# Down-projections in row tiles over four banks, a shorter feature map, and new instruction orders

## The chip, the core and the metric

The kernel runs on one NeuronCore of a Trainium2 chip. Five engines work side by side, each through its own instruction stream in order: TensorE (PE in the profile, its weight loads PEld), VectorE (DVE), ScalarE (ACT), GpSimd (POOL) and SyncE (SP), which issues the DMA transfers. They meet through semaphores. TensorE writes to PSUM, which has eight banks of 128 partitions x 512 fp32 values. The metric is the device time of one execution in microseconds.

## What is computed

One sequence of 2048 tokens of width 512 goes through two branches, which a gate per token mixes. Branch A is attention in four segments of 512 tokens, with 32 heads of width 16 and a memory that is carried from segment to segment; branch B is a gated MLP of width 1792.

```python
g = sigmoid((x * gate_w).sum(-1, keepdims=True))
# branch A, for each of 4 segments, per head (width 16)
p     = softmax(qs @ ks.T * scale + causal mask)
a_dot = p @ vs
phi   = lambda t: where(t > 0, t + 1.0, exp(t))
a_mem = (phi(qs) @ M) / (phi(qs) @ z + 1e-6)
o     = gh * a_mem + (1 - gh) * a_dot          # gh = sigmoid(beta), per head
M, z  = M + phi(ks).T @ vs, z + phi(ks).sum(rows)
a = concat(o) @ wo
# branch B
b = (gelu(x @ w_gate) * (x @ w_up)) @ w_down
out = g * a + (1 - g) * b
```

## The kernel before

**Staging.** All weights are kept in SBUF. Segment s (0 to 3) owns 512 tokens. Its stages are: projections K, Q, V (names `K1_0.2`: segment 1, block 0, piece from contraction block 2 on); gate and up products (`G`, `U`, 14 blocks of 128 features each); scores, exponential and weighted values; the memory; and the down-projection (`D`). A *product* in this document is one matmul of a 128x128 stationary tile with 512 columns. K, Q, V, G, U need four products for a block; a piece is two of them.

**Attention.** Heads lie in four groups of eight; for each tile t of heads (0 to 3), `attention` makes five *fills*: `A0`, `B0`, `A1`, `B1` (two halves of the keys, for the even and the odd head of a pair) and, for even t only, `L` (the low corners). A fill is `qk1_0A0` (segment 1, tile 0, half A, head 0), 8 or 32 matmuls of K=32 in four row groups into the four PSUM banks `X[0..3]` (line 905). One exponential of 128x2048 (`exp…`, ScalarE, line 911) empties the four banks, GpSimd masks the result (`msk…`, line 914), `pv1_0_0` multiplies it with the values in four column tiles, VectorE transposes that (`pvt…`, line 967), and `norm1_0` (lines 979 to 987) divides, transposes and adds it to `oT`. There are 72 fills in all. The memory read of segments 1 to 3, `numx` (line 825), also uses the four X banks in row tiles; `num` adds the last part from `MZbd`; `numd`, `nump`, `numl` (lines 837 to 854) work them up on VectorE, and four transposing DMAs `oTd` bring them into `oT`.

**PSUM.** Four banks are X. The other four (`banks`, names psW) serve everything else: a group of pieces (`Grp`) gets a bank with its first piece and gives it back when its last reader is done.

**Down-projection.** `downs` (line 1056) makes, for each of the four 128-token tiles of a segment, one sum of 18 products: four with `oT` and `wo`, fourteen with `hT` and `wd`. Each sum holds one bank for as long as its pieces `D1_0.0` to `D1_0.16` are spread over the order. `fin` scales by the gate (lines 1098 and 1101) and `out` writes 128 tokens to memory. In the last segment tile 3 uses the X banks instead. `hT` is `gelu(gate) * up`, where `Um` (line 1052) is the multiplication.

**Tile shape.** TensorE runs a product as one 128x128 tile; fills and `numx` as four row tiles of 32x128; `pv` and `mz` as four column tiles. A product that stands between two fills in whose interval a `pv` stands as well is also issued as four column tiles (`column_runs`, line 246, and `mm`, lines 527 to 532: line 530 is the whole product, line 532 the four column tiles).

**Order.** The order on each of the five engines is written out in lists (`ORDER`, line 41). `Sched.schedule` (line 261) walks through these lists, gives out the banks and fixes the order in time; its estimates decide the choice of banks, not the order. `Emitter` turns data dependencies into semaphore waits; a dependency of TensorE on TensorE gets none (lines 390 and 407), because TensorE runs in order.

**Feature map.** `phi_task` (line 722) takes the exponential on ScalarE (line 728, tile `pex`) and then three VectorE steps on 128x1024: `max(t, 0)` (line 731), `min(exp, 1)` (line 733), and their sum (line 735). There are two such tasks for the keys and two for the queries of three segments, twelve in all. **Memory matrix.** `mzbd` masks the accumulated matrix into `MZc` (line 886) and copies its last block in four pieces into the block-diagonal `MZbd` (line 891), whose zeros GpSimd wrote at the start (`consts`, line 653).

Of the kernel before, what the change touches and what calls it, by code (L numbers as in the profile page):

```python
# [26 lines left out]
N_OST = 3  # L27
PSUM_KEYS = ("X", "W")
# [7 lines left out]
DMA_SPARE = 1.6  # L36
LANDING = {
# [67 lines left out]
    ),  # L105
    "dve": (
# [40 lines left out]
class Instr:  # L147
    __slots__ = ("fn", "reads", "writes", "est", "dma_sem", "waits", "deps", "inc", "fence", "wide", "cols")

    def __init__(self, fn, reads=(), writes=(), est=0.1, dma_sem=None):  # L150
# [9 lines left out]
        self.deps = []  # L160
        self.inc = False
        self.fence = False
        self.wide = self.cols = False


class Grp:
# [172 lines left out]
class Emitter:  # L339
# [45 lines left out]
    def finalize(self):  # L385
# [17 lines left out]
        for eng, ins in self.order:  # L403
            req = {}
            for d in ins.deps:
                if d[0] == "c":
                    if d[1] == PE and eng == PE:
                        continue
# [794 lines left out]
```

## Time and profile before

| What | Value |
|---|---|
| Median of 3 runs | 263.48 us (263.07 to 263.88) |
| The profiled execution, its own time | 263.0 us |
| Its span, first to last instruction | 261.8 us |
| TensorE clock granted | 1.00 |
| TensorE busy | 258.5 us, 99% |
| ScalarE busy | 212.2 us, 81% |
| VectorE busy | 195.5 us, 75% |
| GpSimd busy | 105.0 us, 40% |
| The chain that ended last | 97% TensorE |

The busy share of TensorE is not the share in which its array does useful columns: matmuls are pipelined, and their ends in the profile are modelled. In a row of the grouped view, the columns are: line, engine, operation, output<-inputs, shapes, count | busy us, mean ns of one | idle before, and what ended it. In the chain in order of time they are: start, length, piece, all in us. The busy shares in 40 slices show where which engine is loaded; PE stands at 9 nearly throughout:

```profile
PE   8999999999999999999999999999999999999996
PEld 4543445354445434544444444444444434444454
DVE  0789999987988988798896874888874882447543
ACT  3689898999998887988868887688988787768622
```

### The profile page before, as it was taken

Reading aid. Unit: us, or ns where it says so; the run is one execution under the profiler, and the core shown is the slowest. Engines: PE = TensorE matmul, PEld = TensorE weight load, DVE = VectorE, ACT = ScalarE, POOL = GpSimd, SP = SyncE. Lnnn points to the kernel's source line nnn. Section 1 sums busy time; section 2 is a strip of 40 time slices with the busy share of each in tenths; the row PEclk is TensorE's granted clock in tenths of the full one; section 3 lists DMA queues with packets and bytes.
Section 4 is the critical chain, followed back from the end, with each engine's and each line's share of the span. In section 5 each row is a group of like instructions: output and inputs, shape, how many; then the busy total and the mean of one; then the engine's idle time right before and its main releaser. Section 6 shows DMA issues by size and latency. Waiting matters only on the chain.

```text
span 261.8 us, 8784 instructions
## 1 busy us (share of the span) xinstructions
PE 258.5 (99%) x3861; PEld 119.9 (46%) x3861; DVE 195.5 (75%) x371; ACT 212.2 (81%) x185; POOL 105.0 (40%) x256
## 2 busy tenths in 40 slices
PE   8999999999999999999999999999999999999996
PEld 4543445354445434544444444444444434444454
DVE  0789999987988988798896874888874882447543
ACT  3689898999998887988868887688988787768622
POOL 8236760938000183570740171508081045317220
DMA  6992079600009945160000243230001052001002
GB/s 216 325 184 43 4 84 204 222 4 3 0 13 192 263 62 83 27 141 3 0 3 20 48 101 79 24 105 27 18 3 21 3 64 41 3 3 63 23 3 83
DMA packets 32774, 18.33 MB, mean 70 GB/s; under 512 B 20576, under 2 KB 32736, under 8 KB 32736
## 3 DMA queue, kind: packets, MB, share of 16 engines
q1 hardware_dynamic: 31632, 16.73, 30.3%
q10 hardware_dynamic: 1104, 1.05, 1.3%
q8 instruction: 30, 0.49, 0.8%
q14 instruction: 8, 0.07, 0.1%
HBM read 9.84 MB, written 2.10 MB: 46 GB/s over the span
## 4 chain that ended last, share of the span: by engine, by line
PE 97%; DMA 1%; DVE 0%; issue 0%
PE psW L530 59%; PE psW L532 17%; PE psXALL L905 9%; PE psW L953 6%; PE psXALL L532 2%; PE psW L961 1%; DMA hT<-in_A_x_dram 1%; PE psXALL L530 1%; PE psW L872 1%; PE psXALL L825 1%; PE psXALL L632 1%; DVE obf L1084 0%
## 5 line engine op out<-in xcount | busy, mean ns | idle before, releaser
L911 ACT ACTIVATE pt<-psXALL 128x2048 bf16<-128x2048 f32 x64 | 120.1, 1876 | 24.3 <-PE psXALL L905 22.9
L914 POOL TENSOR_SCALAR_AFFINE_SELECT pt<-pt 128x256 bf16<-128x256 bf16 x128 | 57.7, 463 | 91.4 <-ACT pt L911 86.9
L1052 DVE TENSOR_TENSOR hT<-psW,hT 128x512 bf16<-128x512 f32 x56 | 36.7, 681 | 15.7 <-PE psW L530 11.4
L530 PE MATMUL psW<-xT,wg 128*128 128x512 bf16 x192 | 45.7, 379 | 0.0
L530 PE MATMUL psW<-xT,wu 128*128 128x512 bf16 x166 | 41.8, 380 | 0.0
L914 POOL TENSOR_SCALAR_AFFINE_SELECT ptl<-ptl 128x512 bf16<-128x512 bf16 x32 | 23.0, 718 | 44.2 <-ACT ptl L911 42.4
L967 DVE STREAM_TRANSPOSE tb<-psW 128x512 f32<-128x512 f32 x32 | 22.6, 710 | 17.8 <-PE psW L961 17.7
L530 PE MATMUL psW<-wd,hT 128*128 128x512 bf16 x134 | 34.9, 380 | 0.0
L530 PEld LDWEIGHTS psW<-xT,wg 128*128 128x128 bf16 x192 | 18.1, 98 | 21.5 <-issue 0.4
L905 PE MATMUL psXALL<-qT,kpad 32*128 32x320 bf16 (+3 forms) x512 | 25.4, 273 | 0.0
L530 PEld LDWEIGHTS psW<-xT,wu 128*128 128x128 bf16 x166 | 15.1, 98 | 19.1 <-issue 1.9
L532 PE MATMUL psW<-wd,hT 128*32 128x512 bf16 x304 | 20.1, 380 | 0.0
L530 PEld LDWEIGHTS psW<-wd,hT 128*128 128x128 bf16 x134 | 12.5, 98 | 15.6 <-issue 1.7
L953 PE MATMUL psW<-pt,vaug 128*17 128x192 bf16 (+3 forms) x512 | 19.5, 273 | 0.0
L1036 ACT ACTIVATE hT<-psW 128x512 bf16<-128x512 f32 x28 | 15.5, 595 | 4.6 <-PE psW L530 4.6
L905 PEld LDWEIGHTS psXALL<-qT,kpad 32*128 32x128 bf16 x512 | 7.6, 92 | 24.1 <-ACT pt L911 13.6
L812 POOL COPY exsT<-exs 32x4 f32<-32x4 f32 x64 | 14.1, 220 | 8.2 <-ACT exs L803 4.6
L911 ACT ACTIVATE ptl<-psXALL 128x2048 bf16<-128x2048 f32 x8 | 15.0, 1874 | 2.3 <-PE psXALL L905 2.3
L953 PEld LDWEIGHTS psW<-pt,vaug 128*17 128x17 bf16 x512 | 12.2, 91 | 10.0 <-issue 1.2
L530 PE MATMUL psW<-wv,xT 128*128 128x512 bf16 x60 | 16.6, 380 | 0.0
L530 PE MATMUL psW<-xT,wk 128*128 128x512 bf16 (+1 forms) x70 | 15.5, 333 | 0.0
L532 PE MATMUL psW<-xT,wu 128*32 128x512 bf16 x232 | 14.3, 380 | 0.0
(120 smaller groups left out, 358.2 us busy)
## 6 DMA issues: line engine op xcount, KB each, us to landing
out_dram<-ost SPq DMA_DIRECT2D x15, 128.0 KB, 1.9
wg<-in_B_w_gate_dram SPq DMA_DIRECT2D x2, 896.0 KB, 8.1
wu<-in_B_w_up_dram SPq DMA_DIRECT2D x2, 896.0 KB, 6.5
wd<-in_B_w_down_dram SPq DMA_DIRECT2D x2, 896.0 KB, 7.9
phkt<-in_A_x_dram SPq DMA_DIRECT2D x3, 512.0 KB, 5.4
vlow<-vaug SPq DMA_DIRECT2D x8, 136.0 KB, 2.8
hT<-in_A_x_dram SPq DMA_DIRECT2D x2, 256.0 KB, 4.0
wq<-in_A_wq_dram SPq DMA_DIRECT2D x2, 256.0 KB, 5.5
```

Source lines behind the costliest of these rows:

```text
L530: return e.matmul(view(), lhsT, rhs, start=first, stop=last)
L532: r = e.matmul(view()[c:c + 32, :], lhsT[:, c:c + 32], rhs, start=first, stop=last, tile_position=(0, c))
L632: task(f"x0t{nm}_{u}", PE, [Instr(lambda e, k=k, a=a, u=u, k0=k0, src=src: e.transpose(src[:, k, a * 128:(a + 1) * 128], xin[:, 2 * u + a, ...
L812: cross = task(f"exsT{s}", POOL, [Instr(lambda e, g=g, c=c: e.tensor_copy(exsT[sl][32 * g:32 * g + 32, c:16:4], exs[32 * c:32 * c + 32, s4 ...
L825: task(f"numx{s}", PE, [Instr(lambda e, g=g, i=i, qt=qt, t=t: e.matmul(X[g][:, 34 * i:34 * i + 34], phq[32 * g:32 * g + 32, t, qt * 128:(q ...
L905: instrs.append(Instr(lambda e, g=g, lhs=lhs, rhs=rhs, c0=c0, ncol=ncol: e.matmul(X[g][:, c0:c0 + ncol], lhs(32 * g), rhs(32 * g), start=T ...
L911: exp_task(s, f"exp{s}_{t}{name}", [Instr(lambda e: e.activation(dst[:], XALL[:, :].rearrange("p (g c) -> p g c", g=4), ACTF.Exp, scale=AT ...
L914: task(f"msk{s}_{t}{name}", POOL, [Instr(lambda e, view=view, pat=pat, base=base: e.affine_select(out=view, in_=view, compare_op=ALU.is_ge ...
L953: instrs.append(Instr(lambda e, t=t, q=q, kb=kb, slot=slot, c0=c0: e.matmul(gp.f32()[32 * q:32 * q + 17, 128 * kb + 64:512], Vaug[sl][:, k ...
L967: task(f"pvt{s}_{t}_{j}", DVE, [Instr(lambda e: e.transpose(Tb[:, j, :], gp.f32()[:, :]), [gp.key], [("Tb", j)], dve_t(512))], grp=gp)
L1036: lambda e, g=g, ft=ft, s=s: e.activation(hT[s % 2][:, ft, :], g.f32()[:, :], ACTF.Gelu_apprx_tanh),
L1052: task(f"Um{s}_{ft}", DVE, [Instr(lambda e, g=g, ft=ft: e.tensor_tensor(hT[sl][:, ft, :], g.f32()[:, :], hT[sl][:, ft, :], ALU.mult), [g.k ...
```

## The change

1. The down-projections of segments 0 to 2 go through a new function, `row_downs`. For each of the four token tiles the first two products (`D_HEAD`) and the last two (`D_TAIL`) stay whole. Each of the 14 between is cut into four matmuls of K=32, one per row group. Four steps follow each other; in step k row group r works for token tile (r + k) mod 4, so that the four row groups always write four different banks. The first set of steps 1 to 3 waits on TensorE's own semaphore for the previous step's last writes in the same banks (`own`, `hand`), since now two row groups write one bank. All four psW banks are held from the first head to the last `fin`.
2. `phi_task` has two VectorE steps: `max(t, 0) + 1` in one, and the minimum of that and the exponential.
3. `mzbd` makes `MZbd` in one multiplication of the last block with a block mask `blkm`, which GpSimd builds in `consts` (now with five memsets, fenced, and later in GpSimd's order).
4. `ORDER` is new for all engines, and estimates in the schedule are changed. In TensorE's new order the steps `R0.1.2` (segment 0, step 1, from contraction block 2 on; two sets of four) stand in one stretch per segment with fills between them.

The core of the diff:

```diff
+D_HEAD, D_TAIL = 2, 2
...
+    def row_downs(s):
+
+        sl = s % 2
+        gs = tuple(Grp(banks) for _ in range(4))
+
+        def chunk(c, tile):
+            at = slice(tile * 128, (tile + 1) * 128)
+            if c < 4:
+                return oT[sl][:, c, at], wo[:, c, :], [("oT", sl, tile, c), ("w", "wo")]
+            return hT[sl][:, c - 4, at], wd[:, c - 4, :], [("hT", sl, c - 4), ("w", ("wd", (c - 4) // 7))]
+
+        def whole(tile, c0, c1):
+            g = gs[tile]
+            return [mm(g, lambda: g.f32()[:, :], *chunk(c, tile), c == 0, c == 3 + NFT, 512) for c in range(c0, c1)]
+
+        def part(r, tile, c):
+            a, b, rd = chunk(c, tile)
+            return Instr(lambda e: e.matmul(gs[tile].f32()[:, :], a[32 * r:32 * r + 32, :], b[32 * r:32 * r + 32, :],
+                                            start=False, stop=False, tile_position=(32 * r, 0)),
+                         rd, [gs[tile].key], mm_t(512) / 4)
+
+        for tile in range(4):
+            task(f"D{s}_{tile}.0", PE, whole(tile, 0, D_HEAD), grp=gs[tile])
+        c1 = 4 + NFT - D_TAIL
+        for step in range(4):
+            for c in range(D_HEAD, c1, 2):
+                ins = [part(r, (r + step) % 4, cc) for cc in range(c, min(c + 2, c1)) for r in range(4)]
+                t = Task(f"R{s}.{step}.{c}", {PE: ins}, grp=gs)
+                t.tiled, t.row = "qk", True
+                if c == D_HEAD and step > 0:
+                    t.hand = True
+                    for i in ins[:4]:
+                        i.own = True
+                S.add(t)
+        for tile in range(4):
+            task(f"D{s}_{tile}.{c1}", PE, whole(tile, c1, 4 + NFT), grp=gs[tile])
+        for tile in range(4):
+            finish(s, tile, gs[tile])
...
     def downs(s):
+        if not last:
+            return row_downs(s)
...
-                if d[0] == "c" and (d[1] != PE or eng != PE):
+                if d[0] == "c" and (d[1] != PE or eng != PE or ins.own):
...
-                    if d[1] == PE and eng == PE:
+                    if d[1] == PE and eng == PE and not ins.own:
                         continue
...
-            Instr(lambda e: e.tensor_scalar(dst[:, t0:t1, :], src[:, t0:t1, :], 0.0, None, ALU.max), tk, dk,
+            Instr(lambda e: e.tensor_scalar(dst[:, t0:t1, :], src[:, t0:t1, :], 0.0, 1.0, ALU.max, ALU.add), tk, dk,
-            Instr(lambda e: e.tensor_scalar(ex[:], ex[:], 1.0, None, ALU.min), [("pex",)], [("pex",)],
-                  0.5),
-            Instr(lambda e: e.tensor_tensor(dst[:, t0:t1, :], dst[:, t0:t1, :], ex[:], ALU.add),
+            Instr(lambda e: e.tensor_tensor(dst[:, t0:t1, :], dst[:, t0:t1, :], ex[:], ALU.min),
...
-                + [Instr(lambda e, c=c: e.tensor_copy(MZbd[32 * c:32 * c + 32, 34 * c:34 * c + 34],
-                                                      MZc[32 * c:32 * c + 32, 3, :]),
+                + [Instr(lambda e: e.tensor_tensor(
+                    MZbd[:].rearrange("p (c n) -> p c n", c=4), blkm[:],
+                    MZc[:, 3, :].rearrange("p (o n) -> p o n", o=1).to_broadcast([P, 4, 34]), ALU.mult),
```

The new TensorE order around the first row stretch, and its order there before:

```diff
-qk1_0L U1_2.0 V1_2.0 V1_2.2 U1_3.0 U1_2.2 qk1_0A1 U1_3.2 D0_2.0 V2_3.0 V2_3.2 D0_0.0 qk1_0B1 D0_2.2 D0_0.2 U0_10.0 …
+qk1_0L D0_2.0 D0_1.0 D0_3.0 D0_0.0 R0.0.2 qk1_0A1 R0.0.4 R0.0.6 R0.0.8 R0.0.10 R0.0.12 R0.0.14 qk1_0B1 R0.1.2 …
+R0.1.14 qk1_1A0 R0.2.2 … R0.2.14 qk1_1B0 R0.3.2 … R0.3.10 qk1_1A1 R0.3.12 R0.3.14 D0_1.16 D0_2.16 D0_0.16 qk1_1B1
```

More of the change, by code (lines that the diff above doesn't have):

```diff
@@ L36 @@
 DMA_SPARE = 1.6
+OVERLAP = {PE: 0.0, ACT: 0.1, DVE: 0.08, POOL: 0.0, SP: 0.0}
 LANDING = {
@@ L147 @@
 class Instr:
-    __slots__ = ("fn", "reads", "writes", "est", "dma_sem", "waits", "deps", "inc", "fence", "wide", "cols")
+    __slots__ = ("fn", "reads", "writes", "est", "dma_sem", "waits", "deps", "inc", "fence", "wide", "cols", "own")
     def __init__(self, fn, reads=(), writes=(), est=0.1, dma_sem=None):
@@ L162, in __init__ @@
         self.fence = False
-        self.wide = self.cols = False
+        self.wide = self.cols = self.own = False
 class Grp:
@@ L191, in __init__ @@
         self.alts = alts
-        self.grps = () if grp is None else (grp,)
+        self.grps = () if grp is None else grp if isinstance(grp, tuple) else (grp,)
         self.after = tuple(after)
@@ L196, in __init__ @@
         self.tiled = None
+        self.row = self.hand = False
         self.table = None
@@ L259, in column_runs, with change @@
             run = []
+    @staticmethod
+    def change(mode, t):
+        m = "row" if t.row else t.tiled
+        return 0.0 if m == mode else 0.02 if {m, mode} == {"row", "qk"} else SWITCH
     def schedule(self):
@@ L282, in schedule @@
                     continue
-                st = max(cur[e] + (SWITCH if e == PE and t.tiled != mode else 0.0), ready_at[t.id])
+                st = max(cur[e] + (self.change(mode, t) if e == PE else 0.0), ready_at[t.id])
                 if t.grps and t.grps[0].bank is None:
@@ L304, in schedule @@
                     t.finish = st + 2 * t.est[e] if 2 * t.est[e] <= COLD - st else COLD + t.est[e] - (COLD - st) / 2
-                mode = t.tiled
+                mode = "row" if t.row else t.tiled
                 n_ins = sum(8 if i.cols else 2 for i in t.alts[PE])
@@ L313, in schedule @@
                 done += n_ins
-            cur[e] = t.finish
+            cur[e] = t.finish - OVERLAP[e]
             avail = t.finish
@@ L331, in schedule @@
                 npred[s.id] -= 1
-                hop = 0.0 if (e == PE and s.alts.keys() == {PE}) else HOP[e]
+                hop = 0.0 if e == PE and s.alts.keys() == {PE} and not (t.row and s.hand) else HOP[e]
+                if e in (ACT, DVE) and s.alts.keys() == {e}:
+                    hop = 0.02
                 ready_at[s.id] = max(ready_at[s.id], avail + hop)
@@ L477, in _build @@
     MZbd = sb("mzbd", [P, 136])
+    blkm = sb("blkm", [P, 4, 34])
     ident = sb("ident", [P, 128])
@@ L652, in _build @@
          bias=3000.0)
-    task("consts", POOL, [
-        Instr(lambda e: e.memset(MZbd[:], 0.0), writes=[("MZbd",)], est=0.2)]
+    cons = task("consts", POOL, [
+        Instr(lambda e: e.memset(blkm[:], 0.0), writes=[("c", "blk")], est=0.2)]
+        + [Instr(lambda e, c=c: e.memset(blkm[32 * c:32 * c + 32, c, :], 1.0), [("c", "blk")], [("c", "blk")], 0.1)
+           for c in range(4)]
         + [Instr(lambda e, j=j: e.tensor_copy(bdmask[:, j, :], maskc[j][:, 0:1].to_broadcast([P, 17])),
                  [("c", "mask", j)], [("c", "bd", j)], 0.2) for j in range(2)], bias=100.0)
+    for ins in cons.alts[POOL]:
+        ins.fence = True
     exp_tasks = [[] for _ in range(NSEG)]
@@ L730, in phi_task @@
         task(f"{nm}c{s}_{i}", DVE, [
-            Instr(lambda e: e.tensor_scalar(dst[:, t0:t1, :], src[:, t0:t1, :], 0.0, None, ALU.max), tk, dk,
+            Instr(lambda e: e.tensor_scalar(dst[:, t0:t1, :], src[:, t0:t1, :], 0.0, 1.0, ALU.max, ALU.add), tk, dk,
                   0.5),
-            Instr(lambda e: e.tensor_scalar(ex[:], ex[:], 1.0, None, ALU.min), [("pex",)], [("pex",)],
-                  0.5),
-            Instr(lambda e: e.tensor_tensor(dst[:, t0:t1, :], dst[:, t0:t1, :], ex[:], ALU.add),
-                  dk + [("pex",)], dk, 0.79)])
+            Instr(lambda e: e.tensor_tensor(dst[:, t0:t1, :], dst[:, t0:t1, :], ex[:], ALU.min),
+                  dk + [("pex",)], dk, 0.76)])
     def klow_tasks(s, tiles):
@@ L748, in klow_tasks @@
                 ACT: [Instr(lambda e, dst=dst, src=src, j=j: e.activation(dst, src, ACTF.Copy, scale=maskc[j][:, 0:1]),
[L749 removed]
+                            rd, wr, 0.29 + n / 880.0)],
                 DVE: [Instr(lambda e, dst=dst, src=src, j=j: e.tensor_scalar(dst, src, maskc[j][:, 0:1], None, ALU.mult),
@@ L763, in prep @@
                                                               None, ALU.mult),
-                          [("kT", t), ("c", "mask", j)], [("kpad", j, t)], dve_t(512, 4, ap=True))
+                          [("kT", t), ("c", "mask", j)], [("kpad", j, t)], 0.53)
                     for j in ((1,) if first else (0, 1))])
@@ L793, in prep @@
             xt[:, 0:4, :], xt[:, 0:4, :], gwb[:].rearrange("p (o d) -> p o d", o=1).to_broadcast([P, 4, D]),
-            ALU.mult), xkeys + [("w", "gwb")], xkeys, 1.22)])
+            ALU.mult), xkeys + [("w", "gwb")], xkeys, 1.32)])
         for a in range(4):
@@ L819, in prep @@
             exsT[sl][:].rearrange("p (o b) -> p o b", o=1).to_broadcast([P, 8, 16]), ALU.mult),
-            [ek] + [("c", "omgT", g) for g in range(4)], [("GdT", sl)], 0.3)])
+            [ek] + [("c", "omgT", g) for g in range(4)], [("GdT", sl)], 0.38)])
         if s > 0:
@@ L827, in prep @@
                 MZc[32 * g:32 * g + 32, t, :], start=True, stop=True, tile_position=(32 * g, 0)),
-                [("phq", t), ("MZc",)], [("X", g)], 0.0086)
+                [("phq", t), ("MZc",)], [("X", g)], 0.0076)
                 for i, (qt, t) in enumerate(parts[:15]) for g in range(4)]).tiled = "qk"
@@ L843, in prep @@
                          [gn.key, ("exr", s)], [("nd",)], 0.24),
-                   Instr(lambda e: e.reciprocal(ndsc[:], ndsc[:]), [("nd",)], [("nd",)], 0.4)], grp=gn)
+                   Instr(lambda e: e.reciprocal(ndsc[:], ndsc[:]), [("nd",)], [("nd",)], 0.93)], grp=gn)
             ok = phkt[:].rearrange("p a (t h e) -> p (a t) h e", t=4, e=16)
@@ L875, in memory @@
                     start=(kt == 0), stop=(kt == 3), tile_position=(0, 32 * c)),
-                    [("phkt", t), ("Vaug", sl, kt)], [gm.key], 0.0115)
+                    [("phkt", t), ("Vaug", sl, kt)], [gm.key], 0.0079)
                 for t in range(4) for kt in range(4) for c in range(4)], grp=gm)
@@ L890, in memory @@
                 [("MZc",)], 0.33)]
-                + [Instr(lambda e, c=c: e.tensor_copy(MZbd[32 * c:32 * c + 32, 34 * c:34 * c + 34],
-                                                      MZc[32 * c:32 * c + 32, 3, :]),
-                         [("MZc",)], [("MZbd",)], 0.2) for c in range(4)])
+                + [Instr(lambda e: e.tensor_tensor(
+                    MZbd[:].rearrange("p (c n) -> p c n", c=4), blkm[:],
+                    MZc[:, 3, :].rearrange("p (o n) -> p o n", o=1).to_broadcast([P, 4, 34]), ALU.mult),
+                    [("MZc",), ("c", "blk")], [("MZbd",)], 0.28)])
     pt_next = [0]
@@ L907, in fill @@
                             tile_position=(32 * g, 0)), rd, [("X", g)],
-                            (0.018 / len(steps) + ncol / 2370.0 + (0.01 if ncol < 128 else 0.0)) / 4))
+                            (0.006 / len(steps) + ncol / 2370.0 + (0.006 if ncol < 128 else 0.0)) / 4))
                 last_qk[s] = task(f"qk{s}_{t}{name}", PE, instrs)
@@ L967, in pv @@
                 task(f"pvt{s}_{t}_{j}", DVE, [Instr(lambda e: e.transpose(Tb[:, j, :], gp.f32()[:, :]),
-                                                    [gp.key], [("Tb", j)], dve_t(512))], grp=gp)
+                                                    [gp.key], [("Tb", j)], 0.71)], grp=gp)
             def norm():
@@ new lines, in finish @@
+    def finish(s, tile, g):
+        gt = 4 * s + tile
+        ost = ostage[gt % N_OST]
+        rd, wr = [g.key, ("omgt", s)], [("ost", gt % N_OST)]
+        f = S.add(Task(f"fin{s}_{tile}", {
+            ACT: [Instr(lambda e: e.activation(ost[:], g.f32()[:, :], ACTF.Copy, scale=omgt[:, gt:gt + 1]), rd, wr,
+                        act_t(512, ap=True))],
+            DVE: [Instr(lambda e: e.tensor_scalar(ost[:], g.f32()[:, :], omgt[:, gt:gt + 1], None, ALU.mult), rd, wr,
+                        dve_t(512, ap=True))]}, grp=g))
+        if s == NSEG - 2:
+            fins.append(f)
+        dma(f"out{gt}", SP, lambda: out[0, gt * 128:(gt + 1) * 128, :], lambda: ost[:], wr, [("hbm", gt)], 131072,
+            issue=0.47, sm=sem_out[gt])
@@ L1095, in downs @@
             pieces(f"D{s}_{tile}", g, ins, 2, after=dep)
-            rd = [key, ("omgt", s)]
-            f = S.add(Task(f"fin{s}_{tile}", {
-                ACT: [Instr(lambda e, view=view, gt=gt, tile=tile: e.activation(
-                    ostage[(4 * s + tile) % N_OST][:], view(), ACTF.Copy, scale=omgt[:, gt:gt + 1]), rd,
-                    [("ost", (4 * s + tile) % N_OST)], act_t(512, ap=True))],
-                DVE: [Instr(lambda e, view=view, gt=gt, tile=tile: e.tensor_scalar(
-                    ostage[(4 * s + tile) % N_OST][:], view(), omgt[:, gt:gt + 1], None, ALU.mult), rd,
-                    [("ost", (4 * s + tile) % N_OST)], dve_t(512, ap=True))]}, grp=g))
-            if s == NSEG - 2:
-                fins.append(f)
-            dma(f"out{gt}", SP, lambda gt=gt: out[0, gt * 128:(gt + 1) * 128, :],
-                lambda tile=tile: ostage[(4 * s + tile) % N_OST][:], [("ost", (4 * s + tile) % N_OST)], [("hbm", gt)], 131072, issue=0.47, sm=sem_out[gt])
+            finish(s, tile, g)
     fins = []
```

1 line of the change is left out of this document (removed), and 164 rows, old and new, of the table ORDER.

## The prediction

> **What bounds the kernel now.** I read the busy shares and the chain of waits first, then TensorE's waits, then the chain in order of time, which gives the prices of TensorE's work.
>
> ```profile
> PE 258.5 (99%) x3861; PEld 119.9 (46%) x3861; DVE 195.5 (75%) x371; ACT 212.2 (81%) x185; POOL 105.0 (40%) x256
> PE 97%; DMA 1%; DVE 0%; issue 0%
> engine line waited for: us in total, times, longest us
> PE psW L623 <- PEq L1188: 0.8, 1, 0.8
> PE psXALL L632 <- DMA hT<-in_A_x_dram: 0.3, 1, 0.3
> ```
>
> TensorE is busy for 258.5 of 261.8 us and carries 97% of the chain. Its own waits add up to 1.1 us, all in the head. So work taken from VectorE, ScalarE or GpSimd buys nothing by itself; only TensorE's own time counts, and any new wait of TensorE is paid in full. A busy TensorE need not be computing, so I look at the chain in order of time (start, length, piece), where score fills alternate with projections:
>
> ```profile
> 88.28 2.27 PE psW L530 x10
> 90.55 0.33 PE psXALL L905 x8
> 90.88 2.70 PE psW L530 x12
> ...
> 205.45 0.33 PE psXALL L905 x8
> 205.78 2.27 PE psW L530 x10
> 208.05 0.34 PE psXALL L905 x32
> 208.39 2.26 PE psW L530 x10
> 210.65 0.33 PE psXALL L905 x8
> ```
>
> Twelve products take 2.70 us and ten 2.27, so one 512-column product costs 0.215. From 205.45 to 208.05 is one period of 2.60 us: ten products (2.15) and a fill. A fill is 512 columns in four row tiles at once. Were it as fast as a product's 512 columns it would cost 0.215. That leaves 2.60 - 2.15 - 0.215 = 0.235 us, in which no column flows. The tile shape changes twice per period (128x128 to four row tiles of 32x128, and back), so **one change of shape costs about 0.117 us**. That the row tiles do flow at the product's rate is borne out by the fill of 32 small matmuls: eight sets of 64 columns, with four times the weight loads, take 0.34 against 0.33.
>
> Counting shape changes in TensorE's order of instructions before, I get 150: 72 fills and 3 memory reads (line 825) are 75 stretches of row tiles, each entered and left. 150 x 0.117 is 17.6 us, the only sizeable part of TensorE's time that is not columns.
>
> **The change part by part.**
>
> Row tiles for the down-projections. Per segment 0 to 2, 16 full products stay (the first two and last two of each tile's 18) and 56 become 56 sets of four K=32 matmuls: same columns, 168 sets in all. I count the same 1530 column groups (single products or concurrent sets) before and after. What goes is shape changes. In the new order 5, 5 and 6 fills stand inside the three row stretches, so 16 row stretches become 3: 75 become 62, and the changes 150 become 124. 26 x 0.117 = **-3.0 us**.
>
> A row set that *adds* into four banks at once is not in the trace: fills start fresh sums. Its cost is bounded by rows: zero extra from the fills above; the other end is an adding set in another tiling, here 72 column tiles, 18 sets:
>
> ```profile
> 78.07 4.00 PE psW L532 x72
> ```
>
> 4.00/18 is 0.222, so at most 0.007 more per set, 1.2 us for 168. I take zero, because the fills share tiling, banks and weight loads. The Trainium skill ("TensorE: Matmul & The Clock Gate", "Part 3: Packing small matmuls — row/col tiling") speaks against this: it gives a measured speedup of 3.07 for four row tiles at N=512, not 4. By that each set would cost 0.215 x 4/3.07 = 0.28, an estimate from that page, and 168 sets 11 us more; the fills here do not show it.
>
> Hand-overs. In each of the three later steps the first set waits for TensorE's own last write of those banks (nine times). TensorE runs in order, so everything behind waits too, the next fill and thus ScalarE's exponentials included. No row has such a self-wait; the nearest is how soon ScalarE sees a fill finish:
>
> ```profile
> 23.75 0.40 PE L905 MATMUL psXALL<-qT,kpad 32*128 32x320 bf16 x8
> 24.20 1.88 ACT L911 ACTIVATE pt<-psXALL 128x2048 bf16<-128x2048 f32 x1 [0.23 <-PE psXALL L905]
> ```
>
> 0.45 after the fill's start, thus 0.45 - 0.215 = 0.235 after its last column. In eight of nine places a fill (0.215) stands between the last set and the waiting one, so 0.02 to 0.04 stays: **+0.25 us**. Ends: 0 and 9 x 0.235 = 2.1. The cover is the fill; in the ninth place (segment 2, second to third step) there is none, but there the exponential is waited for anyway.
>
> The exponential loop. All scores share one set of four banks, so the next fill waits for the exponential of the last. Its floor:
>
> ```profile
> 44.10 1.87 ACT L911 ACTIVATE ptl<-psXALL 128x2048 bf16<-128x2048 f32 x1
> 46.02 0.40 PE L905 MATMUL psXALL<-qT,kpad 32*128 32x448 bf16 x8
> ```
>
> The exponential ended at 45.97 and the fill began 0.05 later, so the loop is at least 0.45 + 1.88 + 0.05 = 2.38 us. Before, the usual period of 2.60 hid it. A row period with ten sets is 2.15 + 0.215 = 2.37, level with the floor (seven of them: +0.1). Shorter ones stall: the one after the fill 3_0A1 (tile 0, half A, second head of the pair) has eight sets, 1.94, +0.44; the one after 3_2L has eight products, 1.72 + 0.215 + 0.235 = 2.17, +0.21. Other ScalarE work between exponentials overlaps its neighbours by 0.1 and fits into the 12- and 14-set periods. Together **+0.75**; ends 0.55 (a floor 0.05 lower at the last two, nothing at the seven) and 1.45 (0.07 more at ten places where two copies stand between exponentials).
>
> Entry to the row stretches. Four open sums hold all four working banks for 16 products and 56 sets, so nothing can interleave except fills, and the stretch needs the last norm and the last gated product of its segment, both VectorE's:
>
> ```profile
> L1052 DVE TENSOR_TENSOR hT<-psW,hT 128x512 bf16<-128x512 f32 x56 | 36.7, 681 | 15.7 <-PE psW L530 11.4 <-PE psW L532 3.8 <-ACT hT L1025 0.3
> L967 DVE STREAM_TRANSPOSE tb<-psW 128x512 f32<-128x512 f32 x32 | 22.6, 710 | 17.8 <-PE psW L961 17.7
> L983 DVE TENSOR_TENSOR obf<-tb,sc 128x512 bf16<-128x512 f32 x16 | 12.4, 775 | 0.5
> L985 DVE STREAM_TRANSPOSE ott<-obf 128x512 bf16<-128x512 bf16 x12 | 8.5, 711 | 0.4
> L987 DVE TENSOR_TENSOR oT<-oT,ott 128x512 bf16<-128x512 bf16 x12 | 6.1, 506 | 0.7
> L979 DVE RECIPROCAL recip<-tb 128x32 f32<-128x32 f32 x16 | 5.5, 343 | 0.1
> L981 DVE TENSOR_TENSOR sc<-recip,gdT 128x32 f32<-128x32 f32 x16 | 3.5, 221 | 0.6
> L771 DVE TENSOR_SCALAR kpad<-kT,maskc 128x1024 bf16<-128x1024 bf16 x12 | 5.8, 494 | 0.0
> L750 DVE TENSOR_SCALAR klow<-kT,maskc 128x1024 bf16<-128x1024 bf16 x4 | 3.1, 799 | 0.0
> ```
>
> A norm is 0.34 + 0.22 + 0.78 + 0.71 + 0.51 = 2.56 us, in segment 0 without the last. I add up both sides for each entry. Segment 0, from fill 1_0A0: the product pv0_3_0 and its way to VectorE 0.9; a transpose 0.71, seven gated products 4.8, a pad 0.5, two low keys 1.6 and the norm 2.05, together 10.5. TensorE has 24.7 products' worth, ten more, two fills and the four head pairs before its first row set: 42.7 x 0.215 + 3 x 0.215 + 5 x 0.117 = 10.4, so it is level; back-to-back steps overlap a little in the trace, so I charge nothing. Segment 1, from the end of pv1_3_0: VectorE needs 0.24 + 0.71 + 2.56 + 2 x 0.68 = 4.9 until the last bank is free, TensorE gets there after 24 products and a fill, 5.6: in hand. Segment 2, from the end of pv2_3_0: 0.24 + 0.71 + 0.49 + 0.65 + 2.56 + 2 x 0.68 = 6.0 against 26 products and a fill, 5.9: **+0.1**. Ends: 0, and one 0.68 step late at each entry, 2.0.
>
> The queues. SP now issues the first half of wd behind two transposing transfers, which wait for the last step of line 849 on VectorE:
>
> ```profile
> 60.18 0.33 PE psXALL L905 x8
> ...
> 66.18 11.66 ACT L1025 ACTIVATE hT<-hT 128x2048 bf16<-128x2048 bf16 x5
> ...
> 191.10 0.56 PE psXALL L825 x60
> ...
> L849 DVE TENSOR_TENSOR phkt<-psXALL,ndsc 128x480 bf16<-128x480 f32 x12 | 7.6, 650 | 0.1
> ...
> 76.90 2.53 SPq L563 DMA_TRANSPOSE oT<-phkt  x2
> ...
> wd<-in_B_w_down_dram SPq DMA_DIRECT2D x2, 896.0 KB, 7.9
> q8 instruction: 30, 0.49, 0.8%
> ```
>
> Counted from fill 0_3B1 (60.2 before): the large GELU pieces began 6.0 after it, and one copy fewer (0.5) now stands ahead, so two pieces of 1.8 end at 9.1. VectorE then has four gated products, three steps of line 849 and two pads, 5.7, to 14.8. SP's two transfers take 2.5 and wd 7.9: 25.2. TensorE reaches fill 1_0A0 after 64.5 products, a fill and a memory read, 15.0, the row stretch 10.4 later and the first set that reads wd two sets and a fill on, 26.0: nil, with 0.8 in hand. TensorE's matmuls grow from 3861 to 4674, 21%; the instruction queue held 0.8% of 16 engines' span for 30 blocks, 37 would be 1%, and TensorE's waits show none for code: nil.
>
> VectorE's steps. The feature map loses one of three steps (0.525 x 12), the memory matrix four copies for one multiply (12 x 0.173 against 3 x about 0.28):
>
> ```profile
> L733 DVE TENSOR_SCALAR pex<-pex 128x1024 bf16<-128x1024 bf16 x12 | 6.3, 525 | 0.0
> L891 DVE COPY mzbd<-mzc 32x34 bf16<-32x34 bf16 x12 | 2.1, 173 | 0.4
> L886 DVE TENSOR_TENSOR mzc<-mzacc,gbd 128x136 bf16<-128x136 f32 x3 | 0.9, 284 | 0.0
> ```
>
> 6.3 + 2.1 - 0.85 = 7.5 us off VectorE, hidden behind TensorE: nil on the path. GpSimd's constants, four memsets more and moved behind the masks of tile 2, are wanted only before the first memory read, a tile later: nil.
>
> Sum: -3.0 + 0.25 + 0.75 + 0.1 = **-1.9 us**, 261.8 to 259.9 in span. The profiled run took 263.0 with 1.2 us around the span, 0.48 below the median of 263.48, so I take it off the median: 263.48 - 1.9 = **261.6**.
>
> **The rivals.**
>
> *Each row set pays the 0.007 and the hand-overs are dear (no change).* For: neither is in a row. Against: the fills' rate. With hand-overs at half their upper end (+0.8): 261.6 + 1.2 + 0.8 = 263.6: fewer changes of shape, but no gain.
>
> *The entries cost more than the shapes save (slower).* Place: the start of each row stretch, where TensorE has no other work because every bank is held. A norm late by its 2.56 us at all three: +7.7, 269.2; late by 1.6 each: 266.3. It decides from (1.9 + 0.8)/3 = 0.9 us each. For: segments 0 and 2 have nothing in hand by my count, and wd 0.8. Against: VectorE is rid of 7.5 us, and before, all of VectorE's order left TensorE without a wait.
>
> *Adding in four banks runs at a lower rate (slower).* The dearest that a row shows for 512 columns in row tiles is the fill's whole piece of 0.33, with its two changes in it; at that price per set, 168 x 0.115 = +19: 280.9. It decides from 2.7/168 = 0.016 per set. For: no row shows it. Against: fills, and column tiles that do add. The Trainium skill's 3.07 (page and section above) would put it at 272.6, as an estimate.
>
> **How the numbers follow.** Forecast 0.69 (own range 260.4 to 262.7), no change 0.13, late entries 0.12, lower rate 0.06. 0.3% of 263.5 is 0.8 us, about what can be told from no change. Faster 0.69, same 0.13, slower 0.18. The range: low end all stalls nil, 263.48 - 3.0 = 260.4; high end the hand-overs at their upper end (2.1 in place of 0.25) and one late entry (0.7), 261.6 + 1.9 + 0.7 = 264.2.
>
> **What would show it.** Inside a row stretch the fill and sets follow without the 0.117 gap, periods of 2.38 to 2.40 with ten sets; 124 changes; TensorE's waits stay near 1 us plus 0.6 at fills 3_0B1 and 3_2A1; first sets of a step no more than 0.05 late. Sets above 0.23, or gaps of a microsecond before a row stretch, would prove me wrong.

## The result, and the profile after

The changed kernel takes 262.06 us (median of 22 runs) against 263.44 us for the kernel before on the same chip (22 runs): a ratio of 0.9952, interval 0.9937 to 0.9966, so 0.9 to 1.7 us faster. The profiled executions span 260.8 us after and 261.8 us before.

The head of the profile of the changed kernel, and its chain of waits by engine:

```profile
span 260.8 us, 10397 instructions
PE 254.2 (97%) x4653; PEld 127.0 (49%) x4674; DVE 184.2 (71%) x348; ACT 212.2 (81%) x190; POOL 104.6 (40%) x260
...
PE 90%; ACT 3%; DVE 2%; issue 2%; DMA 1%; POOL 1%; ACTq 0%; POOLq 0%
```

TensorE's share of the chain has gone from 97% to 90%; ScalarE and VectorE now stand in it. VectorE is busy 184.2 us in place of 195.5: its two shorter parts alone make that 187.8 (e3_dve_alone below), and the rest comes from the new lists, which also move 44 small tasks (copies, sums, scalings) between ScalarE and VectorE, 21 of them to VectorE and 23 to ScalarE. Of 4674 matmuls 4653 have a record; the missing ones are mostly first products after a stretch of another shape, and the chain shows each as "0.16 issue", which is no idle time.

The chain in order of time (start, length, piece) through the first row stretch of the changed kernel. Line 917 is a fill, line 1085 the row sets, four matmuls each:

```profile
84.85 0.22 PE psXALL L917 x8
85.06 2.59 PE psW L1085 x48
87.65 0.22 PE psXALL L917 x8
87.87 3.13 PE psW L1085 x56
...
94.29 0.22 PE psXALL L917 x8
94.51 2.20 PE psW L1085 x40
```

Twelve sets take 2.59, so a set that adds into four banks costs 0.216, no more than a whole product, and a fill among them costs 0.22 where it cost 0.33 between products. Fourteen sets after a hand-over (87.87) take 3.13 in place of 3.02. So the row tiles do in the trace what they were to do. The other end of the matter is segment 2:

```profile
206.30 0.22 PE psXALL L917 x8
206.51 2.16 PE psW L1085 x40
208.67 0.33 PE psXALL L917 x32
209.00 2.18 PE psW L1085 x40
211.18 0.24 PE psXALL L917 x8
211.43 0.94 PE psW L1085 x16
212.36 0.01 issue
212.38 1.10 PE psW L1085 x16
213.48 0.39 PE psXALL L917 x8
```

At 212.38 stands the hand-over that no fill covers, at 213.48 fill 3_0B1. Two times four sets are 1.73 by the price above; they take 0.94 and 1.10, and the fill 0.39: 0.26 of that is the hand-over, 0.23 the wait for the exponential. The dearest wait in segment 3, at fill 3_2A1, has ScalarE itself in the chain:

```profile
232.31 0.40 PE psXALL L917 x32
...
232.80 1.89 ACT ptl L923
234.69 0.05 issue
234.73 0.40 PE psXALL L917 x8
```

**One number for each run.** The traces differ in their heads: the first fill starts between 13.29 and 13.82 us in the changed kernel and its variants, through the first loads. So I add up, for each trace and from the first fill on, the time from the start of each of TensorE's column groups to the start of the next, less 0.2133 us per 512 columns (columns without a record are counted too). All kernels here have the same columns, so differences of this sum are differences of time. How far two traces agree shows e5_whole_seg2, which has the changed kernel's code up to the row stretch of segment 2: each fill up to there starts within 0.01 us of its twin. Where the expectations below quote such sums, they count from the end of the head and come out up to 0.23 higher (3.55 for 3.32, 0.69 for 0.62, 0.82 for 0.75).

Before, the sum is 21.52 us, after 20.61: **0.91 less**. 26 changes of shape fewer at 0.103 (the median gap at a change in the trace of before; row tiles to products 0.103, products to row tiles 0.099, column tiles to row tiles 0.108) make 2.7, so 1.8 us went elsewhere. Each trace is one execution: those of the kernel before and of e3_dve_alone lie 0.5 and 0.6 us below the medians of their runs, that of the changed kernel 0.1. What the old orders usually lose beyond that stands in no trace here, so comparisons with these two are given by the ratios as well (the medians differ by 1.4 us, the traces by 0.9).

### The profile page after: what moved, and what is told of

The parts are those of the page before. It is cut to its first block, busy times and chain, and to the rows that moved or that the text cites. A ratio compares the mean times of both kernels' runs of the same rounds, so it can differ in the third digit from the quotient of the medians.

```text
span 260.8 us, 10397 instructions
## 1 busy us (share of the span) xinstructions
PE 254.2 (97%) x4653; PEld 127.0 (49%) x4674; DVE 184.2 (71%) x348; ACT 212.2 (81%) x190; POOL 104.6 (40%) x260
## 4 chain that ended last, share of the span: by engine, by line
PE 90%; ACT 3%; DVE 2%; issue 2%; DMA 1%; POOL 1%; ACTq 0%; POOLq 0%
PE psW L539 34%; PE psW L541 24%; PE psW L1085 14%; PE psXALL L917 8%; PE psW L965 5%; ACT pt L923 2%; PE psXALL L541 2%; DMA hT<-in_A_x_dram 1%; PE psXALL L539 1%; PE psW L973 1%; DVE tb L979 1%; ACT ptl L923 1%; PE psXALL L836 1%; DVE hT L1064 0%; PE psXALL L641 0%
## 5 line engine op out<-in xcount | busy, mean ns | idle before, releaser
L1085 PE MATMUL psW<-wd,hT 32*128 32x512 bf16 x576 | 34.8, 374 | 0.0
L539 PE MATMUL psW<-xT,wu 128*128 128x512 bf16 x111 | 28.1, 380 | 1.2 <-issue 0.8
L1114 DVE TENSOR_SCALAR ost<-psW,omgt 128x512 bf16<-128x512 f32 x8 | 5.8, 747 | 32.7 <-PE psW L539 31.1
L539 PE MATMUL psW<-xT,wg 128*128 128x512 bf16 x112 | 28.0, 380 | 0.6 <-issue 0.3
L541 PE MATMUL psW<-xT,wu 128*32 128x512 bf16 x424 | 25.9, 379 | 0.0
L541 PE MATMUL psW<-xT,wg 128*32 128x512 bf16 x432 | 25.4, 379 | 0.0
L1085 PEld LDWEIGHTS psW<-wd,hT 32*128 32x128 bf16 x576 | 18.9, 93 | 10.5
L539 PEld LDWEIGHTS psW<-xT,wg 128*128 128x128 bf16 x116 | 10.5, 98 | 13.0 <-issue 2.1
L541 PEld LDWEIGHTS psW<-xT,wu 128*32 128x32 bf16 x424 | 10.8, 97 | 10.4 <-issue 0.4
L541 PEld LDWEIGHTS psW<-xT,wg 128*32 128x32 bf16 x432 | 10.6, 97 | 10.0 <-issue 0.4
```

Of the source, the lines that this page charges most:

```text
L539: return e.matmul(view(), lhsT, rhs, start=first, stop=last)
L541: r = e.matmul(view()[c:c + 32, :], lhsT[:, c:c + 32], rhs, start=first, stop=last, tile_position=(0, c))
L1085: return Instr(lambda e: e.matmul(gs[tile].f32()[:, :], a[32 * r:32 * r + 32, :], b[32 * r:32 * r + 32, :], start=False, stop=False, tile_ ...
L1114: DVE: [Instr(lambda e: e.tensor_scalar(ost[:], g.f32()[:, :], omgt[:, gt:gt + 1], None, ALU.mult), rd, wr, dve_t(512, ap=True))]}, grp=g))
```

## The experiments

All ratios are against the kernel before, run on the same chip; "beyond columns" is the sum just described. A ratio difference of 0.001 is 0.26 us.

| Run | Ratio (interval) | Beyond columns, us |
|---|---|---|
| before | | 21.52 |
| changed | 0.9952 (0.9937 to 0.9966) | 20.61 |
| e1_whole | 1.0066 (1.0054 to 1.0078) | 23.93 |
| e2_dve_undone | 0.9985 (0.9974 to 0.9997) | 21.63 |
| e3_dve_alone | 1.0008 (0.9989 to 1.0027) | 21.47 |
| e4_more_waits | 1.0057 (1.004 to 1.0074) | 23.23 |
| e5_whole_seg2 | 0.9972 (0.9955 to 0.9989) | 21.23 |
| e6_whole_seg0 | 0.9981 (0.9963 to 0.9999) | 21.36 |
| e9_whole_seg1 | 0.9971 (0.9949 to 0.9992) | 21.21 |
| e7_moved | 0.998 (0.9963 to 0.9997) | 21.61 |
| e8_whole_mz | 1.0056 (1.0034 to 1.0078) | 23.75 |
| e11_norm_late | 1.0032 (1.0014 to 1.005) | 22.94 |

**Row sets as whole products (e1_whole).**

```diff
-                ins = [part(r, (r + step) % 4, cc) for cc in range(c, min(c + 2, c1)) for r in range(4)]
-                t = Task(f"R{s}.{step}.{c}", {PE: ins}, grp=gs)
...
+                S.add(Task(f"R{s}.{step}.{c}", {PE: whole(step, c, c + 2)}, grp=gs))
```

> The changed kernel with its own orders, in which every piece of two row sets is issued as two whole products (128x128 tile) in the same place, so that each step does one tile; no self-wait. 150 changes of tile shape in place of 124, same columns. Theory (the gain is the changes of shape, part of it lost again to waits): 26 changes x 0.103 us (the median gap at a change in the trace of before) = +2.7, less the hand-overs (0.6) and the stalls of the ten-set and eight-set periods (0.4) that go with the row tiles: +1.7, so 263.8 us. That is above the kernel before, because the new orders have waits of their own (about 0.5). Rival (the gain comes from VectorE's shorter steps or from the new orders, row tiles are neutral): 262.1 us, as the changed kernel.

Measured: 265.24 us against 263.6 for the kernel before, 3.32 us more beyond columns than the changed kernel. Both theories missed it, the first by 1.4 us. The chain of this run at the third memory matrix (line 883, 64 small matmuls):

```profile
171.97 0.34 PE psXALL L917 x32
172.31 0.59 PE psW L883 x57
172.91 1.29 issue
174.20 0.22 PE psW L883 x6
```

In the midst of these matmuls, with no semaphore to wait for, TensorE stands still; 1.46 us more than in the changed kernel lie there. Without that piece the sum is 22.47, 1.86 above the changed kernel, and the forecast of +1.7 is near. The runs by segment and e8_whole_mz test that reading.

**Segment by segment (e5_whole_seg2, e6_whole_seg0, e9_whole_seg1).** The same edit under `if s == 2:`, `s == 0` and `s == 1`.

> The changed kernel with whole products in place of the row sets in segment 2 alone (six fills stand inside that stretch: 10 changes of shape come back, 134 in all). Theory: 10 x 0.103 = +1.03 us, less what the row tiles lose there (the uncovered hand-over 0.25, two covered ones 0.07, stalls of the exponential loop 0.09 + 0.03 + 0.23): +0.35 in the profiled span, 262.4 us; so segment 2 gains little. Rival (row tiles are worth a third of what the first run showed in every segment, 3.2 / 3): +1.1, 263.1 us.

> The same in segment 0 alone (five fills inside: 8 changes come back, 132 in all). Theory: 8 x 0.103 = +0.82, less three covered hand-overs (0.11) and 0.06 of the exponential loop: +0.65, 262.7 us. Rival as for segment 2: +1.1, 263.1 us. TensorE's instructions after this stretch stand 168 earlier in its code, so a stop for code like the 1.3 us one of the first run may appear at another place; then it is read off the trace and taken out.

> Whole products in place of the row sets in segment 1 alone (five fills inside the stretch: 8 changes of shape come back, 132 in all). Theory: 8 x 0.103 = +0.82, less two covered hand-overs seen late there (0.07) and the stall of 0.17 at fill 2_0L: +0.6 in the span from the end of the head on, 262.7 us; with the runs of segments 2 and 0 (+0.69 and +0.82 from the head on) the row tiles are then worth 2.1 us, and 3.55 - 2.1 = 1.45 of the first run is the stop without a releaser. Rival (the first run's 3.2 is all the row tiles'): the three segments have to add up to 3.5, so +2.0 here, 264.1 us.

Measured: +0.62, +0.75 and +0.61 beyond columns, together 1.98 (1.8 by the ratios), with no such stop in any of them (0.09 and 0.03 of the last two lie at the third memory matrix, behind the stretch). The first run's 3.32 less its stop is 1.86, and its fills come 0.66, 0.57 and 0.62 later in the three stretches. So **the row tiles are worth 1.9 us**, not 3.2, and the rival that all of the first run's difference is theirs falls. Segment 2 comes back with 0.27 more than I expected; the chain of e5_whole_seg2 shows where:

```profile
211.78 0.36 PE psXALL L917 x8
...
212.22 1.89 ACT pt L923
214.11 0.05 issue
214.16 0.40 PE psXALL L917 x8
```

The period of eight products in that place waits for the exponential as well, 0.28 beyond a plain change of shape; I had counted that wait as one that goes with the row tiles.

**The stop (e8_whole_mz).**

```diff
-qk2_2L mz2 U2_11.0 U2_9.0 U2_11.2 U2_3.0 qk2_2A1 Q3_2.0
+qk2_2L U2_11.0 U2_9.0 U2_11.2 U2_3.0 qk2_2A1 mz2 Q3_2.0
```

(and VectorE's `mzacc2` three tasks later.)

> The first run of this study (all row sets as whole products) with the third memory matrix's 64 small matmuls one fill later, so that TensorE has 1.7 us more work in the stretch of code before the place where it stood still for 1.3 us without a releaser. Theory (TensorE waited for its code there, which belongs to the place of those matmuls in the code, not to the row tiles): the gap is gone, 265.2 - 1.4 = 263.8 us, so that row tiles are worth 1.7. Rival (the 3.2 us belong to the row tiles): 265.2 us.

Measured: 264.92 us. The stop at the third memory matrix is gone, but the time isn't: the moved matmuls brought waits for ScalarE. Its waits and its chain:

```profile
PE psW L541 <- ACT qT L559: 0.6, 1, 0.6
PE psXALL L917 <- ACT ptl L923: 0.2, 1, 0.2
```

```profile
176.95 0.50 ACT qT L559
177.45 0.04 issue
177.50 1.05 PE psW L541 x16
```

So the stop went when the small matmuls were moved, as expected, and the price of the row tiles rests on the three runs by segment, not on this one. That TensorE waited for its own code there is argued only: an instruction transfer ran between 171.4 and 171.6 in the trace of e1_whole, but none while TensorE stood still (172.9 to 174.2), and no row says that TensorE waited for it. The trace of e8_whole_mz also has a shorter stop, 0.4 us at 109.74, ahead of the second memory matrix, where the same code in e1_whole runs through. So the place in the code is not the whole story, and the cause of these stops stays open.

**VectorE's two parts (e3_dve_alone, e2_dve_undone).** The first puts the two-step feature map and the one-step memory matrix into the kernel before; the second takes them out of the changed kernel.

```diff
-            Instr(lambda e: e.tensor_scalar(dst[:, t0:t1, :], src[:, t0:t1, :], 0.0, 1.0, ALU.max, ALU.add), tk, dk,
+            Instr(lambda e: e.tensor_scalar(dst[:, t0:t1, :], src[:, t0:t1, :], 0.0, None, ALU.max), tk, dk,
...
+            Instr(lambda e: e.tensor_scalar(ex[:], ex[:], 1.0, None, ALU.min), [("pex",)], [("pex",)],
...
-            Instr(lambda e: e.tensor_tensor(dst[:, t0:t1, :], dst[:, t0:t1, :], ex[:], ALU.min),
+            Instr(lambda e: e.tensor_tensor(dst[:, t0:t1, :], dst[:, t0:t1, :], ex[:], ALU.add),
```

> The kernel before with VectorE's two parts alone (feature map in two steps, memory matrix in one, GpSimd's constants for it), orders as before. Theory: no change, 263.4 us, within 0.3. Rival (VectorE's steps give the gain): 262.1 us.

> The changed kernel with the feature map in three VectorE steps and the memory matrix in four copies again: 7.5 us more on VectorE, the rest and all orders unchanged. Theory (VectorE's steps are hidden behind TensorE): no change, 262.1 us, within 0.3. Rival (the shorter steps are what lets the row stretches start without a wait): waits of TensorE of 0.5 to 2 us ahead of the row stretches, 262.6 to 264 us.

Measured: in the old orders the parts are worth nothing (ratio 1.0008, 0.05 less beyond columns). In the new orders they are worth 1.02 (0.9 by the ratios). TensorE's program is the same in e2_dve_undone and in the changed kernel, so the start of each matmul can be set against its twin; the lag (behind the head, where it is 0.03) grows in these places:

```
matmul                                    changed   e2     lag
value product of segment 1, after 0_3B1    58.85   59.03   0.18
up product of segment 0                    65.19   65.67   0.48
fill 1_1A0                                 90.77   91.48   0.71
up product of segment 1, after 1_3A0      115.76  116.60   0.84
gate product of segment 2                 124.67  125.65   0.99
```

No single wait is large, and none stands where I had looked for it, at the entry of a row stretch. At fill 1_1A0, inside the first row stretch, ScalarE's rows show the way, first in e2_dve_undone, then in the changed kernel:

```profile
88.60 1.06 ACT L742 ACTIVATE pex<-kT 128x1024 bf16<-128x1024 bf16 x1 [0.89 <-DVE kT L749]
89.56 1.86 ACT L925 ACTIVATE pt<-psXALL 128x2048 bf16<-128x2048 f32 x1
...
87.41 1.06 ACT L741 ACTIVATE pex<-kT 128x1024 bf16<-128x1024 bf16 x1
88.37 1.86 ACT L923 ACTIVATE pt<-psXALL 128x2048 bf16<-128x2048 f32 x1
```

The feature map's exponential writes the tile `pex`, which VectorE's last step of the task before (line 749) still reads. With three steps in place of two that step ends later, ScalarE waits 0.89 us for it, the score exponential behind starts 1.19 us later, and fill 1_1A0 has to wait for that one. The theory is right for the orders before and wrong for the new ones, which spend what VectorE was relieved of.

**The price of a hand-over (e4_more_waits).**

```diff
-                if c == D_HEAD and step > 0:
+                if c == D_HEAD + 2 or c == D_HEAD and step > 0:
                     t.hand = True
```

> The changed kernel with a wait for TensorE's own last write at the second piece of each of the 12 steps as well, 12 waits more, with nothing between the write and the wait. It prices an uncovered hand-over. By the one uncovered hand-over of the changed kernel (0.25 us late): 12 x 0.25 = +3.0, less the exponential's stalls that these waits now cover (0.4): 264.7 us. By the upper end of the prediction (0.235): 264.5. Rival (a hand-over costs 0.04 with or without cover, and the late set there was the exponential loop's): 262.1 + 0.5 = 262.6 us.

Measured: 265.06 us, +2.63 beyond columns. The fills behind a self-wait with nothing between come 0.23 later each (1_1A0, 1_1B0, 2_0B0, 3_0B0), so **0.23 for each uncovered self-wait**. Not all twelve are uncovered: `R0.0.4` stands behind fill 1_0A1 and costs 0.08, and the one ahead of fill 3_0B1 falls into the wait for the exponential and adds 0.07. The chain of this run at the first of them in segment 1:

```profile
143.52 0.58 PE psW L1085 x8
144.10 0.01 issue
144.11 0.70 PE psW L1085 x8
```

Two pieces of two sets, 0.43 each without a wait, take 0.59 and 0.71 here. The rival (0.04 with or without cover) falls. In the changed kernel the eight covered hand-overs are late by 0.00 to 0.04 and 0.23 together.

**The entries (e11_norm_late).**

```diff
+                if t == 3 and s < 3:
+                    ins[2:2] = [Instr(lambda e: e.tensor_tensor(ov, tv[:, :, :, 0:16], rb, ALU.mult),
+                                      [("Tb", 0), ("Tb", 1), ("sc1", i2)], [("obf",)], 0.79) for _ in range(2)]
```

> The changed kernel with the large multiplication of the norm of the last tile done three times in segments 0 to 2, so that VectorE comes 2 x 0.73 = 1.46 us later to what each row stretch waits for; the result is the same. In the changed kernel's trace VectorE is done 0.7, 0.5 and 0.3 us before TensorE needs it at the three entries (segments 0, 1, 2). Theory (a late VectorE is paid in full there, since every bank is held and nothing else can run): 0.75 + 0.95 + 1.15 = +2.85, 264.9 us, with the waits ahead of or in the whole products that open the stretch. Rival (the margins are larger than they look, since VectorE has idle time ahead): +0.3 or less, 262.4 us.

Measured: +2.33 beyond columns. TensorE's waits of this run:

```profile
PE psW L539 <- DVE hT L1067: 0.6, 1, 0.6
PE psW L539 <- DVE qT L562: 0.4, 1, 0.4
PE psW L1088 <- DVE oT L997: 0.4, 1, 0.4
```

All three lie at the entries: the norm itself in segment 0 (line 997 into 1088), the banks behind it in segments 1 and 2. The lag against the changed kernel grows by 0.58, 0.79 and 0.96 there. Of 1.46 us each, 0.9, 0.7 and 0.5 were therefore in hand; past that, a late VectorE is paid in full.

**Two waits taken out by order (e7_moved).**

```diff
-exp2_0A0 pke2_0 exp2_0B0 pke2_1 exp2_0L exp2_0A1
+exp2_0A0 exp2_0B0 pke2_0 exp2_0L pke2_1 exp2_0A1
...
-qk3_2A0 U3_5.0 U3_0.0 U3_0.2 U3_6.0 U3_5.2 U3_6.2 pv3_0_0 qk3_2B0 pv3_0_1 D2_3.16 pv3_1_1 pv3_1_0 qk3_2L U3_4.0
+qk3_2A0 D2_3.16 U3_5.0 U3_0.0 U3_0.2 U3_6.0 U3_5.2 qk3_2B0 U3_6.2 pv3_0_0 pv3_0_1 pv3_1_1 qk3_2L pv3_1_0 U3_4.0
```

(`fin2_3` goes ahead of `exp3_2B0`, and `Um3_4` behind `pvt3_1_0`.)

> The changed kernel with two waits of TensorE for ScalarE taken out by order alone: in segment 2 the two exponentials of the feature map go behind one score exponential more (fill 2_0L was 0.17 late), and in segment 3 the last output copy of segment 2 and its products go ahead of the second tile's exponential, with the product of pt and V one fill later (fill 3_2A1 was 0.31 late). Theory (each wait is on the path): -0.45, 261.6 us, and both fills start without a wait. Rival (the time is lost again at the next wait, since ScalarE's work is what limits there): 262.1 us.

Measured: 1.00 us more beyond columns than the changed kernel, nearly all of it between fills 3_2A0 and 3_2A1. ScalarE's and TensorE's rows of this run, in the view in order of time:

```profile
230.64 1.88 ACT L921 ACTIVATE pt<-psXALL 128x2048 bf16<-128x2048 f32 x1 [1.55 <-PE psW L963]
233.78 1.88 ACT L921 ACTIVATE ptl<-psXALL 128x2048 bf16<-128x2048 f32 x1 [1.26 <-PE psW L971]
...
232.57 0.41 PE L915 MATMUL psXALL<-qT,klow 32*128 32x64 bf16 x32 [0.83 <-ACT pt L921]
```

The exponentials now wait for `pv` (lines 963 and 971), which has to read the old contents of `pt` and `ptl` before they can be written anew: I had moved `pv` later without counting whose buffer it frees. The other half changed nothing: fill 2_0L is still 0.17 late, because exponential 2_0B0 had waited for its fill, not for the feature map's exponential ahead of it. No version tried here beats the changed kernel.

## Why the prediction was right, and where its size was off

- **Changes of shape, -3.0: right, a little too large.** 124 changes and no gap inside a stretch, as forecast. A change costs 0.103, not 0.117, so -2.7: I had divided all 0.235 us of a period that were not columns by its two changes, though some 0.04 of them belong to the fill's second set (0.013) and to the 0.003 that every product takes beyond its columns. The Trainium skill ("TensorEngine Tiling (Array Packing)", "Key Properties") says that a change of tiling mode drains TensorE. The trace has a gap of 0.10 us at each change, which fits it.
- **Adding sets at no extra: right.** 0.216 each. The rival of a lower rate and the Trainium skill's 3.07 ("TensorE: Matmul & The Clock Gate", "Part 3: Packing small matmuls — row/col tiling"), by which a set would take 0.28 (an estimate), are not borne out here. The upper end of 0.222 was read a little too high: the 4.00 us of the 72 column tiles hold a change of shape, and without its 0.10 a set there takes 0.217.
- **Hand-overs, +0.25: right.** 0.23 for the eight covered ones; an uncovered one costs 0.23, the upper end of 0.235 that I had taken from ScalarE's row. The ninth was to cost nothing of its own, since the exponential is waited for anyway: at fill 3_0B1 hand-over and wait make 0.26 + 0.23 = 0.49, where the prediction had 0.44 for the exponential loop.
- **The exponential loop, +0.75: right in place, too small.** 0.49 there, 0.31 at fill 3_2A1 (0.21 forecast), and 0.36 in the ten-set periods (0.1 forecast): 1.16 in all, inside the ends of 0.55 to 1.45. The floor of 2.38 is what one gets when ScalarE starts 0.45 after the fill; where the fill has itself waited, and after an `L` fill of 32 matmuls, the starts of the fills in segment 2's stretch (206.13, 208.56, 211.03, 213.48) are 2.43 to 2.47 apart. That is the term that was mis-sized most among those I priced.
- **Entries, +0.1: nil**, with 0.9, 0.7 and 0.5 us in hand. The mechanism of the rival "late entries" is real (paid in full past the margin) but does not set in; the count had put the margins at 0, 0.7 and -0.1.
- **The queues, nil: right.** The trace of the changed kernel has no wait of TensorE for `wd` or for code.
- **VectorE's steps, nil: right as an addition to the old orders, wrong in the new.** The forecast of 7.5 us off VectorE holds (7.7 in e3_dve_alone), but in the new orders these steps cover 1.0 us of waits. The prediction's reason, that TensorE's waits of before show none for VectorE, holds only for the orders of before.
- **What the sum left out: the new orders away from the row stretches.** By the traces, e3_dve_alone to e1_whole without its stop is 21.47 to 22.47, +1.0 for the orders alone. By the ratios it is +0.1 (-0.5 to +0.7), since the traced execution of e3_dve_alone lies below its median; so their cost is known only to lie between these bounds. The prediction charged them only fill 3_2A1. In the changed kernel I find, beyond the terms above, fills 0_3A1 (+0.16) and 1_0B0 (+0.10) and three smaller ones (0.04 to 0.05) late behind ScalarE, and a product late behind VectorE by 0.11: 0.5 in all. Ahead of 0_3A1 ScalarE started an exponential 0.82 after its fill in place of 0.45; the profile names GpSimd's line 693, which now runs there. In e2_dve_undone, where GpSimd runs the same work 0.3 us later, that exponential is on time and the next one starts 0.81 after its fill. So the delay goes with GpSimd's work, but what it waits for stays open.

Added up: -2.7 + 0.2 + 1.2 + 0.5 = -0.8, against -0.91 in the trace (waits of before that are gone make up part of the rest), where the prediction had -1.9. By undoing, the row tiles with their waits are worth 1.9; the prediction's own terms for them (-3.0, 0.25, 0.54 of the loop, 0.1) give 2.1. So the forecast of the main edit held.

The whole came out at -1.4 us by the medians, near the forecast of -1.9, and that is in part luck. Without VectorE's two parts, which the sum put at nil, the change gains only 0.4 us (e2_dve_undone, 0.1 to 0.7 by its ratio). They made up for waits of the new orders that the sum had left out as well.

## What to carry to other kernels

Where TensorE sets the end, count its changes of tile shape: at 0.10 us each they are worth removing, by giving work beside small matmuls their shape, if it fills the array. What that buys is limited by the next loop behind it: take the floor of the loop (fill, exponential, fill) from several of its turns, the late ones too, before saying what a shorter period saves. And when a change comes with new orders, treat the orders as an edit of their own: cost each period in them, and don't carry over from the old orders that an engine has slack.

## What the runs showed of the hardware

- Four K=32 row sets of 512 columns that add into four banks follow each other every 0.216 us. After a hand-over the four matmuls of a set no longer start within 0.01 us, but spread over 0.07 (91.03, 91.06, 91.09, 91.10 in the changed kernel), and the sets behind keep that spread without losing rate (the next four start 0.22 to 0.23 later).
- TensorE's wait for its own last write costs 0.23 us with nothing between, and 0.00 to 0.04 behind a fill of 512 columns.
- A stop of 1.3 us without any releaser came among small matmuls (57 of them in 0.59 us) when 336 matmuls fewer stood ahead of them in the code, and was gone with eight products and a fill more ahead of them. A stop of 0.4 us came in that last run (e8_whole_mz) at another place, where the same code had run through in e1_whole.
